# Attention with mixed heads: keys and queries stored once, two heads on the halves of the array

## The chip, the cores and the metric

One core of one Trainium2 chip runs the whole program as one launch. The core has a matrix array (TensorE, PE in the profile; its weight loads are PEld), VectorE (DVE), ScalarE (ACT), GpSimd (POOL), a queue engine that issues transfers (SyncE, SP), and 16 DMA engines. The metric is device time in microseconds, the median of repeated runs. The kernel before takes 1551.23 us (three runs, 1547.59 to 1551.54).

## The reference

Four batches, twelve heads, 448 positions, 64 values a head. Scores are mixed across heads before the softmax, probabilities after it; the result passes through two feed-forward parts.

```
scores = matmul(q, k.T) / 8
scores = einsum('bhij,hg->bgij', scores, w_pre)
attn = exp(scores - max(scores))
attn = attn / (sum(attn) + 1e-9)
attn = einsum('bhij,hg->bgij', attn, w_post)
x = matmul(attn, v)                      # then heads side by side: (1792, 768)
h = x @ w_in                             # 768 -> 2048
x = (h * cos(h)) @ w_out                 # 2048 -> 768
out = (silu(x @ w_gate) * (x @ w_val)) @ w_out2
```

## The kernel before

The 448 query rows of a batch are cut into four chunks of 12, 12, 11 and 10 blocks; a block holds ten query positions for all twelve heads, 120 rows. Work goes by blocks (45 a batch, 180 in all), and for each block there are steps: `premix` multiplies the scores of the block's 120 rows with w_pre (`psm`), `rowmax`, `expo`, `den` and `rec` make the softmax, `norm_hi` and `norm_lo` store it as two half-precision numbers `eh` and `el`, `post` mixes heads again and transposes (`psa`), `at_hi` and `at_lo` store that as high and low half, `at0` and `at1`.

While one chunk goes through these steps, the scores of the next chunk are made head by head (`qk`, tile `pss`), copied to a buffer `s` by ScalarE (`spread`, L201) and sent by a transfer to the rows of `x` where the next chunk's premix reads them (L202). There are three buffers `s` and two banks for `pss`. The product with v (`pv`, tile `psv`) follows seven blocks behind the end of its chunk.

To keep precision, every operand stands as high and low part. For the scores a key tile holds one head: the high part on that head's 64 rows, the low part on the other 64 (`hi_k`, L105, `lo_k`, L110). Queries come from memory twice, on both halves of the rows, so that one matmul over 128 rows sums high and low part of k; the high part of q (`qh`) and its low part (`ql`) each give one matmul (L190), two a head. `qh` is written by a casting transfer from GpSimd's queue (L126) beside the plain one from SP's (L125); `ql` is computed by GpSimd (L135). For the product with v one weight tile holds the high and the low part of one head's v, 128 columns, and eight matmuls a head (L287) leave two sums on two halves of the rows. `pv_out` moves both by ScalarE (L304, L305), adds them on GpSimd (L307) and stores them (L308).

The order on each engine is written out: a plan gives each step a block number, and within a block the kinds of steps stand in the order of one tuple of names, `order`. Steps of the next chunk are put at block s0 + h * (n - 2) // 12 for head h, where s0 is the chunk's first block and n its number of blocks. Engines take their instructions in that order. After the last chunk the feed-forward class takes over; the first pieces of it are planned into the last chunk.

Of the kernel before, what the change touches and what calls it, by code (L numbers as in the profile page):

```python
# [30 lines left out]
def f(ap):  # L31
    return ap.bitcast(F32)


def attention(ctx, tc, qT, kT, vN, mix, xs, ff):
# [9 lines left out]
    p_k = pool("a_k", 13, SB, scores, "right")  # L45
# [54 lines left out]
    def half(h):  # L100
        return slice(64 * (h % 2), 64 * (h % 2) + 64)

    def hi_k(b, h, copy=nc.scalar.copy):
        t = ktiles[b, h] = p_k.tile([128, S], F32R, tag="k", name=f"k_{b}_{h}")
        copy(t[half(h)], raws["k", b, h // 2][half(h)])  # L105

    def lo_k(b, h, eng=nc.gpsimd):

        t = ktiles[b, h]
        eng.tensor_tensor(t[half(h + 1)], raws["k", b, h // 2][half(h)], f(t[half(h)]), op=ALU.subtract)  # L110

    def dma_q(b, c, hh, early=()):

        src = qT[b, c, hh].rearrange("d (e i) -> d e i", e=6)
        if 0 in early or not early:
            hi = p_q.tile([128, 6, 120], F32R, tag="qh", name=f"qh_{b}_{c}_{hh}")
            lo = p_q.tile([128, 6, 120], F32R, tag="ql", name=f"ql_{b}_{c}_{hh}")
            raw = p_q.tile([128, 6, 120], F32, tag="qr", bufs=2, name=f"qr_{b}_{c}_{hh}")
            qtiles[b, c, hh] = hi, lo
            raws["q", b, c, hh] = raw  # L120
        for e in early:
            s = slice(3 * e, 3 * e + 3)
            nc.sync.dma_start(raws["q", b, c, hh][:, s], src[:, s])
        if not early:
            nc.sync.dma_start(raw, src)  # L125
            nc.gpsimd.dma_start(hi, src)  # L126
# [41 lines left out]
    def split_v(b, jc, part):  # L168

        r = raws["v", "r", b, jc]  # L170
        rv = r.rearrange("p (m e d) -> p m e d", e=2, d=D)
        by = vscale[b][0][:112, 1:2]
        if part == 0:
            nc.scalar.activation(r, r, AF.Copy, scale=by)
        elif part == 1:
            t = vtiles[b, jc] = p_v.tile([112, 6, 4, D], F16, tag="v", name=f"v_{b}_{jc}")
            nc.vector.tensor_copy(t[:, :, 0::3], rv)
        else:
            e, t = part - 2, vtiles[b, jc]
            nc.gpsimd.tensor_tensor(t[:, :, 1 + e], rv[:, :, e], t[:, :, 3 * e], op=ALU.subtract)  # L180

    X, SP, SMALL, PM, E, EHL, PA, AT, PV, XO = ({} for _ in range(10))

    def qk(b, c, h, place=(ps_s, "s")):

        n = CH[c]
        hi, lo = qtiles[b, c, h // 6]
        ps = place[0].tile([128, 512], F32, tag=place[1], name=f"pss_{b}_{c}_{h}")
# [4 lines left out]
        SP[b, c, h] = ps  # L193
# [84 lines left out]
    def pv(b, c, h):  # L278

        n = 10 * CH[c]  # L280
        if h % 4 == 0:
            PV[b, c, h // 4] = ps_v.tile([128, 4, 128], F32, tag="pv", name=f"psv_{b}_{c}_{h}")
        ps = PV[b, c, h // 4]
        for jc in range(4):
# [7 lines left out]
    def pv_out(b, c, g4, par):  # L292

        n = 10 * CH[c]
        if par == 0:
            XO[b, c, g4] = p_o.tile(
                [128, 2, n], F32, tag="xo", padded_shape=[128, 2, 120], bufs=3, name=f"xo_{b}_{c}_{g4}"
            ), p_o.tile([128, 2, 120], F32, tag="xt", name=f"xt_{b}_{c}_{g4}")
        x, t = XO[b, c, g4]
        ps = PV[b, c, g4]  # L300
        und = vscale[b][1]
        own = slice(64 * par, 64 * par + 64)
        off = slice(64 - 64 * par, 128 - 64 * par)
        nc.scalar.activation(t[own, :, :n], ps[off, par::2, :n], AF.Copy, scale=und[own])  # L304
        nc.scalar.activation(x[own], ps[own, par::2, :n], AF.Copy, scale=und[own])  # L305
        if par == 1:
            nc.gpsimd.tensor_tensor(x, x, t[:, :, :n], op=ALU.add)  # L307
            nc.sync.dma_start(  # L308
                xs[b][:, 2 * g4:2 * g4 + 2, COFF[c]:COFF[c] + CREAL[c]], x[:, :, :CREAL[c]]
            )  # L310
# [6 lines left out]
    def at(i, fn, *a):  # L317
        plan.setdefault((i, fn.__name__), []).append((fn, a))
# [6 lines left out]
    for ci, (b, c) in enumerate(chunks):  # L325
        n, s0 = CH[c], first[b, c]
        if ci + 1 < len(chunks):
            nb, ncn = chunks[ci + 1]
            for h in range(12):
                i = s0 + h * (n - 2) // 12  # L330
                at(i, qk, nb, ncn, h)
                at(i + 1, spread, nb, ncn, h)
            for hh in range(2 if ci else 0):
                i = s0 - 6 + 4 * hh
                at(i, dma_q, nb, ncn, hh)
                for e in range(2):
# [28 lines left out]
        for h in range(12):  # L365
            i = s0 + n + 7 + h * (nn - 2) // 12
            at(i, pv, b, c, h)
            if h % 4 == 3:
                for par in range(2):
                    at(i + 1 + par, pv_out, b, c, h // 4, par)  # L370
# [4 lines left out]
    order = ("at_hi","l1_part","post","spread","dma_v","w_bits","hidden","den","rowmax","rec","norm_hi","dma_k","x_dma","w_dma","pv_out","at_lo","norm_lo","lo_k","dma_q","max_v","w_shift","lo_q","split_v","x_lo","premix","scale_v","w_split","expo","x_hi","qk","hi_k","pv")  # L375


    with tc.manual_schedule():
        vec, act, pl = nc.vector, nc.scalar, nc.gpsimd
        dma_q(0, 0, 0, range(1))  # L380
        for m in range(6):
            dma_k(0, m, p_fk)
            if m == 1:
                dma_q(0, 0, 0, range(1, 2))
            if m == 3:
                dma_q(0, 0, 1, range(2))
        hi_q(0, 0, 0, 0, vec.tensor_copy)
        lo_q(0, 0, 0, 0, vec)
        for h in range(0, 12, 2):
            for k in (h, h + 1):  # L390
                hi_k(0, k, act.copy if k == 1 else vec.tensor_copy)
            if h == 0:
                hi_q(0, 0, 0, 1, act.copy)
            for k in (h, h + 1):
                lo_k(0, k, pl if k in (3, 5, 9, 11) else vec)
            if h == 0:
                lo_q(0, 0, 0, 1)
            if h == 4:
                for e in range(2):
                    lo_q(0, 0, 1, e)  # L400
            for k in (h, h + 1):
                qk(0, 0, k, ((ps_s, "s"), (ps_a, "a"), (ps_m, "m"))[k % 3])
                spread(0, 0, k, p_fk, 12)
                if k == 3:
                    nc.sync.dma_start(mix_sb, mix)
                if k in (1, 2):
                    hi_q(0, 0, 1, k - 1, act.copy)
# [13 lines left out]
        p_o = pool("a_o", 2)  # L421
# [285 lines left out]
def _layout(inputs):  # L707
# [21 lines left out]
    def bits(w):  # L729
# [4 lines left out]
        "qT": np.concatenate([qT, qT], 3).reshape(B, 4, 2, 128, 720),  # L734
# [31 lines left out]
```

## Time and profile before

| | |
|---|---|
| median of three runs | 1551.23 us |
| profiled execution | 1546.38 us, span 1544.6 us |
| array (PE) busy | 1457.5 us (94%) |
| VectorE busy | 985.5 us (64%) |
| ScalarE busy | 731.2 us (47%) |
| GpSimd busy | 712.8 us (46%) |
| mean granted clock of the array | 0.993 of full speed |

The shares are means over two stages that differ: attention up to about 510 us, where all engines are loaded, and the feed-forward part, where the array is nearly always busy. Rows of a stretch or of a place in time tell more than the totals. The array's matmuls are pipelined, so the shown durations overlap, and the distance between starts is what one costs.

### The profile page before, as it was taken

To read this page: it belongs to the slowest core of one execution; us is meant where nothing else is said; L and a number is where in the kernel's file an instruction comes from. 1 tells how busy PE (TensorE), PEld (TensorE's weight loads), DVE (VectorE), ACT (ScalarE), POOL (GpSimd) and SP (SyncE) were. 2 spreads that over 40 slices of the span, in tenths; PEclk is the share of its full clock that TensorE was granted. 3 is DMA by queue.
4 is the path that set the end of the run, shared out by engine and by line. 5 is a ranking of instruction groups with operands and counts; after the bars stand their busy time and mean duration, and the time that the engine had idled before them with its cause. 6 is when DMAs were issued, how large, how long until landed. Compare 5 with 4: busy or idle time off the path is not lost.

```text
span 1544.6 us, 25392 instructions
## 1 busy us (share of the span) xinstructions
PE 1457.5 (94%) x9346; PEld 1239.7 (80%) x9346; DVE 985.5 (64%) x1966; ACT 731.2 (47%) x1579; POOL 712.8 (46%) x658
## 2 busy tenths in 40 slices
PE   5898898998898899999999999999999999999999
PEld 3566666666666779999999998998998989899898
DVE  6987878887788785757767766833336263542613
ACT  4788888888788773322322323533313131221310
POOL 3888889889787752322423323213213131321310
PEclk9999999999999999999999999999999999999999
DMA  6666567556644541212202211211203030120202
GB/s 205 162 189 177 162 173 199 169 157 196 178 129 142 140 134 60 62 41 62 62 30 73 62 42 41 62 41 53 71 2 102 21 102 21 53 71 1 72 37 108
DMA packets 100589, 149.19 MB, mean 97 GB/s; under 512 B 19856, under 2 KB 82544, under 8 KB 100464
## 3 DMA queue, kind: packets, MB, share of 16 engines
q1 hardware_dynamic: 96432, 137.24, 30.4%
q0 software_dynamic: 4032, 10.32, 2.6%
q8 instruction: 74, 1.21, 0.3%
q14 instruction: 51, 0.42, 0.1%
HBM read 97.81 MB, written 11.01 MB: 70 GB/s over the span
## 4 chain that ended last, share of the span: by engine, by line
PE 68%; DVE 12%; DMA 8%; ACT 6%; issue 3%; POOL 2%; SPq 1%; ACTq 0%; POOLq 0%
PE ph L592 11%; PE ph L593 11%; PE ph L594 11%; PE py L638 8%; PE py L639 8%; PE py L640 8%; DMA x<-s 5%; PE psm L206 4%; PE pss L190 3%; PE psv L287 2%; DVE el L242 2%; DVE sm L211 1%; ACT e L219 1%; POOL l_i L532 1%; DMA qr<-in_qT 1%
## 5 line engine op out<-in xcount | busy, mean ns | idle before, releaser
L616 POOL TENSOR_TENSOR gl<-r,gh 128x448 fp32r<-128x448 f32 x112 | 133.9, 1196 | 495.9 <-ACT gh L615 465.8
L592 PE MATMUL ph<-x,h_i 128*128 128x448 f32 x960 | 352.3, 367 | 0.0
L593 PE MATMUL ph<-x,h_i 128*128 128x448 f32 x960 | 351.1, 366 | 1.2 <-POOL x L572 1.2
L594 PE MATMUL ph<-x,l_i 128*128 128x448 f32 x960 | 351.1, 366 | 0.2 <-POOL l_i L532 0.2
L638 PE MATMUL py<-gh,h_o 128*128 128x448 f32 x672 | 249.7, 372 | 12.2 <-DVE acc L644 7.9
L640 PE MATMUL py<-gh,l_o 128*128 128x448 f32 x672 | 247.5, 368 | 0.6 <-POOL l_o L532 0.6
L639 PE MATMUL py<-gl,h_o 128*128 128x448 f32 x672 | 247.4, 368 | 0.0
L235 POOL TENSOR_SCALAR eh<-e,sm 120x448 f16<-120x448 f32 x180 | 216.4, 1202 | 62.2 <-DVE sm L230 29.0
L644 DVE TENSOR_TENSOR acc<-py,acc 128x448 f32<-128x448 f32 x288 | 176.0, 620 | 88.1 <-PE py L640 87.8
L206 PE MATMUL psm<-x,wpre_sb 120*120 120x448 f32 x360 | 180.9, 585 | 39.8 <-ACT e L219 28.8
L593 PEld LDWEIGHTS ph<-x,h_i 128*128 128x128 f32 x960 | 180.5, 188 | 17.0 <-POOL x L572 1.6
L592 PEld LDWEIGHTS ph<-x,h_i 128*128 128x128 f32 x960 | 180.5, 188 | 15.3 <-issue 0.4
L594 PEld LDWEIGHTS ph<-x,l_i 128*128 128x128 f32 x960 | 180.4, 188 | 15.4 <-POOL l_i L532 0.6
L614 DVE TENSOR_TENSOR r<-ph,r 128x448 f32<-128x448 f32 x48 | 29.9, 623 | 200.7 <-PE ph L594 200.5
L638 PEld LDWEIGHTS py<-gh,h_o 128*128 128x128 f32 x672 | 126.2, 188 | 31.7 <-DVE acc L644 13.3
L532 POOL TENSOR_TENSOR l_i<-f_i,h_i 128x384 fp32r<-128x384 f32 x80 | 87.6, 1102 | 137.8 <-ACT h_i L531 137.8
L242 DVE SCALAR_TENSOR_TENSOR el<-e,sm,eh 120x448 f16<-120x448 f32 x180 | 141.0, 783 | 9.6 <-POOL eh L235 9.6
L615 ACT CAST gh<-r 128x448 fp32r<-128x448 f32 x112 | 63.4, 566 | 174.4 <-DVE r L614 136.4
L255 PE MATMUL psa<-wpost,eh 120*112 120x120 f16 x720 | 126.3, 218 | 14.3 <-DVE at L276 12.9
L640 PEld LDWEIGHTS py<-gh,l_o 128*128 128x128 f32 x672 | 126.4, 188 | 13.2 <-POOL l_o L532 1.4
L639 PEld LDWEIGHTS py<-gl,h_o 128*128 128x128 f32 x672 | 126.4, 188 | 11.3
L190 PE MATMUL pss<-k,qh 128*120 128x448 f32 (+2 forms) x192 | 122.6, 639 | 11.3 <-DVE k L110 7.4
(88 smaller groups left out, 2680.9 us busy)
## 6 DMA issues: line engine op xcount, KB each, us to landing
r_o<-in_w_out SPq DMA_DIRECT2D x56, 384.0 KB
x<-s SPq DMA_DIRECT2D x96, 210.0 KB
r_i<-in_w_in SPq DMA_DIRECT2D x32, 384.0 KB
qh<-in_qT POOLq DMA_DIRECT2D x28, 360.0 KB, 4.9
qr<-in_qT SPq DMA_DIRECT2D x28, 360.0 KB
x<-s SPq DMA_DIRECT2D x48, 192.5 KB
r_i<-in_w_gate SPq DMA_DIRECT2D x24, 384.0 KB
r_i<-in_w_val SPq DMA_DIRECT2D x24, 384.0 KB
```

The costliest lines, as they stand in the source:

```text
L190: nc.tensor.matmul(ps[:10 * n, :S], qq[:, h % 6, :10 * n], ktiles[b, h], start=(i == 0), stop=(i == 1))
L206: nc.tensor.matmul(ps[:120, :S], wpre_sb, X[b, c][:120, k], start=True, stop=True)
L235: nc.gpsimd.tensor_scalar(eh, E[b, c, k], sm[:, 3:4], 1.0, op0=ALU.mult, op1=ALU.mult)
L242: nc.vector.scalar_tensor_tensor(el, E.pop((b, c, k)), sm[:, 3:4], eh, op0=ALU.mult, op1=ALU.subtract)
L592: nc.tensor.matmul(ps, wh, xh, start=(kk == 0), stop=False)
L593: nc.tensor.matmul(ps, wh, xl, start=False, stop=False)
L594: nc.tensor.matmul(ps, wl, xh, start=False, stop=(kk == 5))
L616: nc.gpsimd.tensor_tensor(gl, r, f(gh), op=ALU.subtract)
L638: nc.tensor.matmul(ps, wh, gh[:, e], start=(e == 0), stop=False)
L639: nc.tensor.matmul(ps, wh, gl[:, e], start=False, stop=False)
L640: nc.tensor.matmul(ps, wl, gh[:, e], start=False, stop=(e == 1))
L644: nc.vector.tensor_tensor(acc[:, m], ps, acc[:, m], op=ALU.add)
```

## The change

Keys lie once as a high tile and a low tile of 128 rows, two heads on the halves (`k0`, `k1`), and queries likewise (`q0`, `q1`); queries are read from memory once. For a pair of heads the scores are three products (high with high, low q with high k, high q with low k), each as two matmuls over 64 rows, one a head, on the two halves of the array's rows. The product with v takes three products instead of four (low with low is left out), each as two matmuls with 64 columns, one a head, on the two halves of the array's columns. Both halves of a pair's result so stand where they are stored, `pv_out` is one activation for three pairs, and the addition is gone. The plan goes by pairs, and the cast of the queries' high part (`hi_q`) is now on VectorE.

```diff
-    p_k = pool("a_k", 13, SB, scores, "right")
+    p_k = pool("a_k", 7, SB, scores, "right")
...
+    def hi_k(b, m, copy=nc.scalar.copy):
+        t = ktiles[b, m] = tuple(
+            p_k.tile([128, S], F32R, tag=f"k{z}", name=f"k{z}_{b}_{m}") for z in range(2)
+        )
+        copy(t[0], raws["k", b, m])
+    def lo_k(b, m, eng=nc.gpsimd):
+        hi, lo = ktiles[b, m]
+        eng.tensor_tensor(lo, raws.pop(("k", b, m)), f(hi), op=ALU.subtract)
+    def dma_q(b, c, parts=(slice(0, 6),)):
...
+        for s in parts:
+            nc.sync.dma_start(raws["q", b, c][:, s], src[:, s])
+    def hi_q(b, c, e, copy=nc.vector.tensor_copy):
...
-        for i, qq in enumerate((hi, lo)):
-            nc.tensor.matmul(
-                ps[:10 * n, :S], qq[:, h % 6, :10 * n], ktiles[b, h], start=(i == 0), stop=(i == 1)
-            )
+        for i, (zq, zk) in enumerate(((0, 0), (1, 0), (0, 1))):
+            for e in range(2):
+                r = slice(64 * e, 64 * e + 64)
+                nc.tensor.matmul(
+                    SP[b, c, 2 * m + e][:n, :S], qtiles[b, c][zq][r, m, :n], ktiles[b, m][zk][r],
+                    start=(i == 0), stop=(i == 2),
+                )
...
-            vt = vtiles[b, jc][:, h // 2, 2 * (h % 2):2 * (h % 2) + 2]
-            for z in range(2):
+        prods = [(jc, zv, za) for jc in range(4) for zv, za in ((0, 0), (0, 1), (1, 0))]
+        for i, (jc, zv, za) in enumerate(prods):
+            for e in range(2):
                 nc.tensor.matmul(
-                    ps[:, h % 4, :n].rearrange("p (k i) -> p k i", i=10), vt, AT[b, c][z][:, :, jc * H + h],
-                    start=(jc == 0 and z == 0), stop=(jc == 3 and z == 1),
+                    ps[64 * e:64 * e + 64, m % 3, :n].rearrange("p (k i) -> p k i", i=10),
+                    vtiles[b, jc][:, m, e, zv], AT[b, c][za][:, :, jc * H + 2 * m + e],
+                    start=(i == 0), stop=(i == len(prods) - 1),
                 )
...
-        nc.scalar.activation(t[own, :, :n], ps[off, par::2, :n], AF.Copy, scale=und[own])
-        nc.scalar.activation(x[own], ps[own, par::2, :n], AF.Copy, scale=und[own])
-        if par == 1:
-            nc.gpsimd.tensor_tensor(x, x, t[:, :, :n], op=ALU.add)
+        nc.scalar.activation(x, PV.pop((b, c, g3))[:, :3, :n], AF.Copy, scale=vscale[b][1])
...
-            for h in range(12):
-                i = s0 + h * (n - 2) // 12
-                at(i, qk, nb, ncn, h)
-                at(i + 1, spread, nb, ncn, h)
-            for hh in range(2 if ci else 0):
-                i = s0 - 6 + 4 * hh
-                at(i, dma_q, nb, ncn, hh)
+            for m in range(6):
+                i = s0 + m * (n - 2) // 6
+                at(i, qk, nb, ncn, m)
                 for e in range(2):
-                    at(i + 3 + e, lo_q, nb, ncn, hh, e)
+                    at(i + 1, spread, nb, ncn, 2 * m + e)
+            if ci:
+                at(s0 - 6, dma_q, nb, ncn)
+                for e in range(2):
+                    at(s0 - 3 + e, hi_q, nb, ncn, e)
+                    at(s0 - 2 + e, lo_q, nb, ncn, e)
...
-        for hh in range(2):
-            for e in range(2):
-                hi_q(0, 1, hh, e, act.copy)
-                lo_q(0, 1, hh, e)
+        dma_q(0, 1)
+        for e in range(2):
+            hi_q(0, 1, e)
+            lo_q(0, 1, e)
...
-        "qT": np.concatenate([qT, qT], 3).reshape(B, 4, 2, 128, 720),
+        "qT": qT.reshape(B, 4, 128, 720),
```

On the array, in block 1 of chunk 1 of the second batch, the kernel before has after the premix one head of the next chunk's scores and then a head's product with v (names carry batch, chunk and head or block, then a running number):

```order
L206 MATMUL psm_1_1_1_2845<-x_1_1_2245,wpre_sb_269 120x448
L190 MATMUL pss_1_2_2_2849<-k_1_2_1466,qh_1_2_0_2509 110x448
L190 MATMUL pss_1_2_2_2849<-k_1_2_1466,ql_1_2_0_2510 110x448
L287 LDWEIGHTS v_0_0_574
L287 MATMUL psv_0_3_8_2852<-at0_0_3_1988,v_0_0_574 128x100
L287 LDWEIGHTS v_0_0_574
L287 MATMUL psv_0_3_8_2852<-at1_0_3_1989,v_0_0_574 128x100
```

In the same place the changed kernel has a pair of heads, in turn (`k0` and `q0` are high parts, `k1` and `q1` low ones; `psv_0_3_3` begins with pair 3):

```order
L202 MATMUL psm_1_1_1_2957<-x_1_1_2322,wpre_sb_250 120x448
L186 MATMUL pss_1_2_2_2961<-k0_1_1_1495,q0_1_2_2597 110x448
L186 MATMUL pss_1_2_3_2962<-k0_1_1_1495,q0_1_2_2597 110x448
L186 MATMUL pss_1_2_2_2961<-k0_1_1_1495,q1_1_2_2598 110x448
L186 MATMUL pss_1_2_3_2962<-k0_1_1_1495,q1_1_2_2598 110x448
L186 MATMUL pss_1_2_2_2961<-k1_1_1_1496,q0_1_2_2597 110x448
L186 MATMUL pss_1_2_3_2962<-k1_1_1_1496,q0_1_2_2597 110x448
L284 LDWEIGHTS v_0_0_571
L284 MATMUL psv_0_3_3_2900<-at0_0_3_2049,v_0_0_571 64x100
```

Two matmuls for one head have become six for two heads, which write two banks in turn, and the matmuls with v write 64 rows instead of 128. Blocks without a pair have neither.

On ScalarE, in blocks 2 and 3 of chunk 0 of the same batch, one score copy stood in each block, with two activations that move results out:

```order
L219 ACTIVATE e_1_0_0_2268,sm_1_0_0_2253<-psm_1_0_0_2213,sm_1_0_0_2253 120x448
L268 ACTIVATE at0_0_3_1988<-psa_0_3_6_2232 112x480
L201 COPY s_1_1_2_2303<-pss_1_1_2_2270 120x448
L304 ACTIVATE xt_0_2_1_2313<-psv_0_2_4_2177,und_0_469 64x2x110
L305 ACTIVATE xo_0_2_1_2312<-psv_0_2_4_2177,und_0_469 64x2x110
L219 ACTIVATE e_1_0_1_2322,sm_1_0_1_2307<-psm_1_0_1_2266,sm_1_0_1_2307 120x448
L268 ACTIVATE at0_0_3_1988<-psa_0_3_7_2290 112x480
L201 COPY s_1_1_3_2350<-pss_1_1_3_2324 120x448
```

Now both copies of a pair stand in one block, and a block without a pair has none:

```order
L215 ACTIVATE e_1_0_0_2340,sm_1_0_0_2330<-psm_1_0_0_2296,sm_1_0_0_2330 120x448
L264 ACTIVATE at0_0_3_2049<-psa_0_3_6_2309 112x480
L197 COPY s_1_1_2_2389<-pss_1_1_2_2342 120x448
L197 COPY s_1_1_3_2392<-pss_1_1_3_2343 120x448
L215 ACTIVATE e_1_0_1_2406,sm_1_0_1_2396<-psm_1_0_1_2338,sm_1_0_1_2396 120x448
L264 ACTIVATE at0_0_3_2049<-psa_0_3_7_2376 112x480
L215 ACTIVATE e_1_0_2_2457,sm_1_0_2_2447<-psm_1_0_2_2404,sm_1_0_2_2447 120x448
```

Two copies have moved together in front of one `exp`, and the results of the product with v come out later, as one activation for six heads.

## Rows read from the trace of the kernel before

**Rows 1.** Busy time by stretch: the second batch, and after attention.
```profile
core 0: us, PE busy (x) PEld busy (x) DVE busy (x) ACT busy (x) POOL busy (x), PEclk, DMA share, GB/s
...
147.14:268.32 121.18, 108.52 (x1117) 78.18 (x1114) 98.23 (x242) 103.91 (x247) 106.52 (x101) 1.00 0.62 176
...
510.46:1544.60 1034.14, 1014.80 (x5109) 924.99 (x5106) 571.74 (x971) 321.00 (x613) 296.85 (x263) 1.00 0.20 59
```

**Rows 2.** Who waited for whom, 60 to 510 us: total, times, longest.
```profile
DVE sm L226 <- ACT e L219: 53.8, 70, 3.3
...
PE psm L206 <- ACT e L219: 24.7, 24, 3.4
...
ACT s L201 <- DMA x<-s: 23.6, 17, 3.4
```

**Rows 3.** The array in order of time, one block: start, duration.
```profile
202.47 0.97 PE L206 MATMUL psm<-x,wpre_sb 120*120 120x448 f32 x2
202.93 0.72 PE L190 MATMUL pss<-k,qh 128*110 128x448 f32 x1
203.49 0.37 PE L190 MATMUL pss<-k,ql 128*110 128x448 f32 x1
203.70 0.60 PE L287 MATMUL psv<-at,v 112*128 112x120 f16 x8
204.14 0.22 PE L255 MATMUL psa<-wpost,eh 120*112 120x120 f16 x1
...
204.77 0.97 PE L206 MATMUL psm<-x,wpre_sb 120*120 120x448 f32 x2
205.57 0.59 PE L287 MATMUL psv<-at,v 112*128 112x120 f16 x8
```

**Rows 4.** Longest chain pieces, 60 to 510 us, and a ScalarE copy that waited.
```profile
133.04 7.04 DMA x<-s
164.65 7.99 DMA qr<-in_qT
198.88 6.17 DMA x<-s
...
205.15 0.53 ACT L201 COPY s<-pss 110x448 f32<-110x448 f32 x1 [1.88 <-DMA x<-s]
```

**Rows 5.** Weight loads by shape: busy, mean ns of one, idle before.
```profile
L255 PEld LDWEIGHTS <-eh 120*112 120x112 f16 x720 | 94.1, 131 | 19.2 <-issue 11.5 <-POOL l_i L532 1.9 <-POOL v L180 1.8
L287 PEld LDWEIGHTS <-v 112*128 112x128 f16 x1536 | 82.4, 97 | 42.8 <-issue 42.8
...
L190 PEld LDWEIGHTS pss<-k,qh 128*120 128x120 f32 x96 | 19.2, 200 | 33.7 <-issue 10.6 <-ACT s L201 9.7 <-DVE k L110 6.5
```

**Rows 6.** ScalarE, GpSimd and VectorE by shape: busy, mean ns of one.
```profile
L268 ACT ACTIVATE at<-psa 112x480 f16<-112x480 f32 x180 | 101.5, 564 | 0.5
...
L305 ACT ACTIVATE xo<-psv,und 64x240 f32<-64x240 f32 x48 | 21.9, 456 | 0.6
L105 ACT CAST k<-kr 64x448 fp32r<-64x448 f32 x37 | 20.6, 558 | 2.3 <-DMA kr<-in_kT 1.8
...
L135 POOL TENSOR_TENSOR ql<-qr,qh 128x360 fp32r<-128x360 f32 x63 | 63.4, 1009 | 25.1 <-ACT qh L130 14.8 <-DMA qr<-in_qT 5.3 <-PE psa L257 1.5
L110 POOL TENSOR_TENSOR k<-kr,k 64x448 fp32r<-64x448 f32 x40 | 55.1, 1377 | 6.2 <-issue 2.1 <-DVE k L105 1.1
L126 POOL DMA_DIRECT2D qh<-in_qT x28 | 16.9, 604 | 0.0
L307 POOL TENSOR_TENSOR xo<-xo,xt 128x240 f32<-128x240 f32 x24 | 16.7, 697 | 1.0 <-ACT xo L305 1.0
...
L130 DVE CAST qh<-qr 128x360 fp32r<-128x360 f32 x1 | 0.3, 347 | 2.0 <-DMA qr<-in_qT 2.0
```

**Rows 7.** VectorE in order of time, start of the program.
```profile
30.92 0.95 DVE L147 TENSOR_REDUCE vmx<-vm 112x1 f32<-112x768 f32 x1 [8.18 <-DMA vm<-in_vN]
```

More of the change, by code (lines that the diff above doesn't have):

```diff
@@ L98, in dma_k @@
         raws["k", b, m] = r
[L100 to L126, printed above, removed]
@@ new lines, in lo_k @@
+    def lo_k(b, m, eng=nc.gpsimd):
+        hi, lo = ktiles[b, m]
+        eng.tensor_tensor(lo, raws.pop(("k", b, m)), f(hi), op=ALU.subtract)
+    def dma_q(b, c, parts=(slice(0, 6),)):
+        if parts[0].start == 0:
+            qtiles[b, c] = tuple(
+                p_q.tile([128, 6, 120], F32R, tag=f"q{z}", name=f"q{z}_{b}_{c}") for z in range(2)
+            )
+            raws["q", b, c] = p_q.tile([128, 6, 120], F32, tag="qr", bufs=2, name=f"qr_{b}_{c}")
+        src = qT[b, c].rearrange("d (m i) -> d m i", m=6)
+        for s in parts:
+            nc.sync.dma_start(raws["q", b, c][:, s], src[:, s])
@@ L137, in dma_v, with lo_q @@
+    def hi_q(b, c, e, copy=nc.vector.tensor_copy):
+        s = slice(3 * e, 3 * e + 3)
+        copy(qtiles[b, c][0][:, s], raws["q", b, c][:, s])
+    def lo_q(b, c, e, eng=nc.gpsimd):
+        hi, lo = (t[:, 3 * e:3 * e + 3] for t in qtiles[b, c])
+        eng.tensor_tensor(lo, raws["q", b, c][:, 3 * e:3 * e + 3], f(hi), op=ALU.subtract)
     def dma_v(b, jc, why):
@@ L276, in at_lo, with pv @@
         nc.vector.scalar_tensor_tensor(tl, src, 2.0 ** -4, th, op0=ALU.mult, op1=ALU.subtract)
-    def pv(b, c, h):
+    def pv(b, c, m):
         n = 10 * CH[c]
[L281 to L284, printed above, removed]
-            vt = vtiles[b, jc][:, h // 2, 2 * (h % 2):2 * (h % 2) + 2]
-            for z in range(2):
+        if m % 3 == 0:
+            PV[b, c, m // 3] = ps_v.tile([128, 4, 128], F32, tag="pv", name=f"psv_{b}_{c}_{m}")
+        ps = PV[b, c, m // 3]
+        prods = [(jc, zv, za) for jc in range(4) for zv, za in ((0, 0), (0, 1), (1, 0))]
+        for i, (jc, zv, za) in enumerate(prods):
+            for e in range(2):
@@ L364, in attention @@
         nn = CH[chunks[ci + 1][1]] if ci + 1 < len(chunks) else 12
[L365 to L370, printed above, removed]
+        for m in range(6):
+            i = s0 + n + 7 + m * (nn - 2) // 6
+            at(i, pv, b, c, m)
+            if m % 3 == 2:
+                at(i + 1, pv_out, b, c, m // 3)
     for i, fn, *a in ff.early_plan(first[B - 1, 3]):
@@ L373, in attention @@
         at(i, fn, *a)
-    order = ("at_hi","l1_part","post","spread","dma_v","w_bits","hidden","den","rowmax","rec","norm_hi","dma_k","x_dma","w_dma","pv_out","at_lo","norm_lo","lo_k","dma_q","max_v","w_shift","lo_q","split_v","x_lo","premix","scale_v","w_split","expo","x_hi","qk","hi_k","pv")
+    order = ("at_hi","l1_part","post","spread","dma_v","w_bits","hidden","den","rowmax","rec","norm_hi","dma_k","x_dma","w_dma","pv_out","at_lo","norm_lo","lo_k","dma_q","max_v","w_shift","lo_q","split_v","x_lo","premix","scale_v","w_split","expo","x_hi","qk","hi_k","hi_q","pv")
@@ L378, in attention @@
     with tc.manual_schedule():
         vec, act, pl = nc.vector, nc.scalar, nc.gpsimd
-        dma_q(0, 0, 0, range(1))
-        for m in range(6):
[L382 to L398, printed above, removed]
-                for e in range(2):
[L400 to L407, printed above, removed]
@@ L408, in attention @@
-        for hh in range(2):
-            dma_q(0, 1, hh, range(2))
-        for hh in range(2):
-            for e in range(2):
-                hi_q(0, 1, hh, e, act.copy)
-                lo_q(0, 1, hh, e)
+        dma_k(0, 0, p_fk)
+        dma_q(0, 0, (slice(0, 3),))
+        dma_k(0, 1, p_fk)
+        dma_q(0, 0, (slice(3, 6),))
+        for m in range(2, 6):
+            dma_k(0, m, p_fk)
+        nc.sync.dma_start(mix_sb, mix)
+        places = (ps_s, "s"), (ps_a, "a"), (ps_m, "m")
+        for m in range(6):
+            hi_k(0, m, act.copy if m % 2 else vec.tensor_copy)
+            if m == 0:
+                hi_q(0, 0, 0, act.copy)
+                lo_q(0, 0, 0, vec)
+            lo_k(0, m, pl if m % 2 else vec)
+            if m == 0:
+                hi_q(0, 0, 1, act.copy)
+                lo_q(0, 0, 1, pl)
+            qk(0, 0, m, places)
+            for e in range(2):
+                spread(0, 0, 2 * m + e, p_fk, 12)
@@ L414, in attention @@
+        dma_q(0, 1)
+        for e in range(2):
+            hi_q(0, 1, e)
+            lo_q(0, 1, e)
         wpre_sb = const.tile([120, 120], F32, name="wpre_sb")
@@ L714, in _layout @@
         n, g = CREAL[c], CH[c]
-        part = np.zeros((B, 2, 6, 10 * g, D), q.dtype)
-        part[:, :, :, :n] = q[:, :, COFF[c]:COFF[c] + n].reshape(B, 2, 6, n, D)
-        part = part.reshape(B, 2, 6, g, 10, D).transpose(0, 1, 5, 2, 4, 3)
+        part = np.zeros((B, 6, 2, 10 * g, D), q.dtype)
+        part[:, :, :, :n] = q[:, :, COFF[c]:COFF[c] + n].reshape(B, 6, 2, n, D)
+        part = part.reshape(B, 6, 2, g, 10, D).transpose(0, 2, 5, 1, 4, 3)
         qT[:, c, :, :, :, :10 * g] = part.reshape(B, 2, D, 6, 10 * g)
```

57 lines of the change are left out of this document (21 added, 36 removed).

## The prediction

> **What bounds the kernel now.** I began with busy time by stretch. The 1544.6 us fall into a start, four batches of attention that end at 510.46 us (the second is a row, 121.2 us, so some 485 us for all) and the feed-forward part behind it. In the last part the array is busy for 1014.8 of 1034.1 us, and the change touches none of its lines, so all must happen in the first 510 us. In a batch of 121.2 us no engine is full: array 108.5, ScalarE 103.9, GpSimd 106.5, VectorE 98.2, the DMA engines at 0.62 [rows 1]. Then the list of waits: VectorE stands 53.8 us until ScalarE's `exp` has ended, the array 24.7 us for the same `exp`, ScalarE 23.6 us (17 times) until a spread transfer has freed a buffer [rows 2]. So the engines pass a delay round among them, and the order in time must say which of them paces an undisturbed block.
>
> It is the array. From one `psm` to the next lie 2.30 us without a gap: 0.80 for the premix (204.77 to 205.57, where no qk stands between), 0.43 for the two qk matmuls of a head (1.23 from `psm` to `psv`, less 0.80), 0.44 for the eight matmuls with v of a head, 0.63 for the twelve of `post` [rows 3]. Starts are used here, since the durations overlap. A qk matmul so takes 0.215 us, one with v 0.055. A batch has 45 blocks and 48 heads of each product: 45 x 1.43 + 48 x 0.87 = 106.1 us. The other 15.1 of 121.2 us are disturbed blocks, above all long transfers: the longest pieces of the chain are a spread of 7.04 us and one of queries of 7.99 us [rows 4].
>
> **The change, part by part.** *Scores.* Two heads had four matmuls over 128 rows; now they have six over 64, in turn on the upper and the lower half. Nothing in this trace has two matmuls beside each other, so I bound them from both sides: beside each other 3 x 0.215 = 0.65 us a pair, one after another 6 x 0.215 = 1.29, against 0.86 now. The weight loads of one half must also run beside those of the other: a load takes 0.20 us [rows 5], which fits one to a step of 0.215, not two.
>
> *Product with v.* Two heads had 16 matmuls with 128 columns, now 24 with 64. Beside each other 12 x 0.055 = 0.66 us, one after another 1.32, against 0.88. The load again: 128 columns took 97 ns, 112 columns of the same type 131 ns, and yet the latter keep a step of 0.0525 us (twelve in 0.63) [rows 3, 5]. So the wide load is the quicker one, and 64 columns may not have that speed. The Trainium skill, TensorEngine Tiling (Array Packing), Restrictions, says that splitting the columns switches the fast weight load off; the trace agrees as far as its narrower load is slower. If a load's share of a step goes with its width, two loads of 64 columns ask 2 x 0.0525 x 64/112 = 0.060 us a step, and a pair costs 0.72 us, not 0.66: 1.4 us more a batch. I take 0.66.
>
> For both products I take the lower bound, as the halves share no rows of the array in the one case and no columns in the other, and no operand waits on the other half's result: -0.43 us a pair, 24 pairs a batch, -10.4: array 95.7 us. The upper bound is +0.87 a pair, +20.9: 127.0.
>
> *ScalarE.* Moving results out goes from 48 activations a batch of 0.456 to 8 over 128x360; the nearest rows are that 0.456 (240 elements) and 0.564 (480), so 0.51: 21.9 - 4.1 = -17.8. Key casts go from 12 of 0.558 to 6, of the same 448 elements: -3.3. ScalarE: 103.9 to 83 [rows 1, 6].
>
> *GpSimd.* Low parts of queries 16 to 8 a batch at 1.01 (-8.1), of keys 12 to 6 at 1.377 (-8.3), 12 additions of 0.70 (-8.4) and 8 issues of 0.604 (-4.8) go: 106.5 to 77 [rows 1, 6].
>
> *VectorE* takes on the query casts, 8 a batch. The one such cast in the trace took 0.347; beside GpSimd it may take twice that. I take 0.5: 98.2 to 102 (101 to 104) [rows 1, 6]. The cast waits for the query transfer, issued three blocks (some 6.9 us) earlier; behind it stand the next block's `den` and `rowmax`, for which `exp` waits. A transfer of 7.99 us would cost 1.1 us there. I take nothing, since such lengths should go: queries shrink from four transfers of 360 KB a chunk to one, 4.4 MB a batch of 176 GB/s x 121 us = 21 MB, a fifth [rows 1, 4].
>
> *Start.* Casts of chunk 1's queries now stand on VectorE ahead of the scaling of w_pre, so the first premix waits for that transfer. The copies ahead of it are done sooner, and VectorE idled 8.18 us there for v [rows 7]. I take 0, with 2 us either way.
>
> *The sum.* The largest load is then VectorE's 102 us, the array's 95.7 next. VectorE idles 23.0 us a batch now, mostly behind ScalarE and long transfers. Both get lighter by a fifth, so I keep half of it, 11.5: a batch takes 113.5, 7.7 less. If all of it went, 19 less; if none, 4 more. Four batches: -31 us. The profiled execution took 1546.4 us, so 1515.4; the median of before stands 4.9 higher, so I forecast **1520 us**, with 1503 to 1538 as this case's own range (a third to two thirds of the idle time kept, 2 us for the start).
>
> **Rivals.** *One after another.* The halves don't overlap, in matmuls or in loads, so the change doesn't do what it says. In the array's queue a pair then takes 2.61 us where 1.74 stand now; the array has 127.0 us a batch, and with half of today's 15.1 us of waits 134.5: +13.3 x 4 = +53, **1604 us**. For it speaks that no pair overlaps in this trace and that a step leaves no room for two loads. It decides from about 2.05 us a pair: 106.1 + 24 x 0.31 + 7.5 is today's 121. If only the scores overlap, a pair takes 0.65 + 1.32 = 1.97, the batch 119.2, the time **1543 us**.
>
> *A stop at each change of shape.* A matmul of `post` is shown for 0.22 us at steps of 0.0525, so 0.165 us of it lies under its successors [rows 3]. If the array had to run empty whenever whole, row-halved and column-halved matmuls follow each other, some 20 times a chunk, that is 3.3 us a chunk or 13 a batch: the array is back at 109, and only the relief of the others is left, half of the 15 us of waits: 116.5, -4.7 x 4 = -19, **1532 us**. No row of before has two shapes, so none speaks against it. The Trainium skill, TensorEngine Tiling (Array Packing), Key Properties, states this drain; no run so far shows it.
>
> *Three buffers for spreads that come in pairs.* Before, copy h+3 waited for the transfer of copy h some 2.5 blocks, or 5.8 us, back. Now both heads of a pair are copied in one block; where pairs stand one block apart (11 times a batch, by the division in the plan) it waits for one 2.3 + 0.4 us back. A spread of 6.17 us already held ScalarE for 1.88 us [rows 4]. With some 5 us each, ScalarE stands 2.2 us 11 times: its load is 83 + 24 = 107, more than VectorE's 102. With the same 11.5 us of idle time a batch takes 118.5 us, -2.7 x 4 = -11, **1540 us**. Against it: only 17 copies waited before.
>
> **How the numbers follow.** Side by side as forecast 0.52; a stop at each change 0.13; spread buffers 0.12; only the scores overlap 0.08; one after another 0.15. A measurement of this kernel tells about 0.3% from no change, 4.7 us. Of the first four I count 0.51, 0.12, 0.05 and 0.03 as faster, together 0.71; 0.01, 0.01, 0.05 and 0.03 as the same, 0.10; slower are 0.02 of the third, 0.02 of the fourth and all of the last, 0.19. The range runs from 1497, below which I see 0.05, to 1570, which leaves out most of the last case.
>
> **What would show it.** In order of time, two `pss` of a pair should start almost together, a `psm` with a pair of qk behind it should be followed after 0.80 + 0.65 us, and a pair with v should take 0.66. If the starts are 0.2 and 0.05 us apart, the halves run one after another. Gaps of some 0.17 us at each change of shape mean the stop. VectorE's wait for `exp` should halve; ScalarE's wait for the spread transfer should not exceed 24 us, or the buffers are the price. The forecast is wrong if a batch takes over 118 us.

## The result, and the profile after

The changed kernel takes 1530.08 us (median of four runs, 1526.95 to 1531.48) against 1551.38 us of the kernel before in the same session: a ratio of 0.9857, 95% interval 0.9831 to 0.9883, so 1.4% faster. The forecast was 1520 us with a range of 1497 to 1570. The profiled execution took 1526.95 us, its span 1525.2 us, 19.4 us less than before.

Busy time by stretch, the second batch and what follows attention, in the columns of [rows 1]:

```profile
core 0: us, PE busy (x) PEld busy (x) DVE busy (x) ACT busy (x) POOL busy (x), PEclk, DMA share, GB/s
...
148.31:262.65 114.34, 108.86 (x1356) 69.71 (x1354) 97.39 (x250) 84.47 (x201) 83.56 (x68) 0.99 0.51 148
...
489.78:1525.20 1035.42, 1013.40 (x5181) 923.32 (x5178) 573.47 (x971) 312.55 (x593) 293.36 (x257) 1.00 0.20 59
```

The batch went from 121.2 to 114.3 us, while the array's busy time stayed at 108.9 (108.5 before). It was busy for 90% of the batch and is now for 95%: the array does no less, it waits less. ScalarE lost 19.4 us, GpSimd 23.0, and the transfers fell from 176 to 148 GB/s. From the first premix to the end of attention the four batches take 459.2 us instead of 483.9 (-24.7); the start is 4.1 us longer and the rest 1.3 us, which together make up the 19.4 us.

The array in order of time, in the place that answers to [rows 3] (start, duration; equal instructions in a row are one line):

```profile
211.97 0.97 PE L202 MATMUL psm<-x,wpre_sb 120*120 120x448 f32 x2
212.87 0.85 PE L186 MATMUL pss<-k,q 64*100 64x448 f32 x6
213.65 0.83 PE L284 MATMUL psv<-at,v 112*64 112x120 f16 x24
214.41 0.26 PE L251 MATMUL psa<-wpost,eh 120*112 120x120 f16 x1
214.50 0.22 PE L252 MATMUL psa<-wpost,eh 120*112 120x120 f16 x1
214.56 0.22 PE L253 MATMUL psa<-wpost,el 120*112 120x120 f16 x1
...
215.08 0.97 PE L202 MATMUL psm<-x,wpre_sb 120*120 120x448 f32 x2
215.89 0.22 PE L251 MATMUL psa<-wpost,eh 120*112 120x120 f16 x1
```

Inside the six `pss` the two heads start 3 ns apart; the second two come 0.28 us later and the third two 0.20 (212.87, 213.15, 213.36), so that the first step holds a part of the stop. Inside the 24 `psv` two start at most 5 ns apart, with a step of 0.052 after a first one of 0.079. So the halves do run beside each other. But the pair of scores takes 0.78 us (212.87 to 213.65) where three steps make 0.61, the pair with v 0.76 (213.65 to 214.41) where twelve make 0.63, premix is followed by `pss` after 0.90 us and by `psa` after 0.81 (215.08 to 215.89), and the first `psa` keeps the second waiting 0.09 instead of 0.05. The whole block takes 3.11 us, an empty one 1.43: the two pairs cost 1.68 us, where one pair each cost 0.86 + 0.88 = 1.74 before. In blocks with one pair alone it costs 0.92 (scores) or 0.90 (v). Taken one by one, a change costs 0.09 us behind a premix (0.90 for 0.81), and the rest of the 0.92 or 0.90 lies in the first step of the pair and between the pair and the first two `psa`.

The weight loads of the same stretch show what happens at a change (idle time before the first of a row in brackets):

```profile
212.87 0.45 PEld L186 LDWEIGHTS pss<-k,q 64*100 64x100 f32 x6 [0.66 <-ACT at L264]
213.65 0.67 PEld L284 LDWEIGHTS <-v 112*64 112x64 f16 x24 [0.33 <-issue]
214.41 0.13 PEld L251 LDWEIGHTS <-eh 120*112 120x112 f16 x1
```

The first load of a new shape starts in the same hundredth as its matmul, and ahead of the scores and of v the load side stood idle: no load is taken ahead across these changes. In the kernel before, where no shape changes, the first load of v behind a premix came 0.37 us ahead of its matmul (205.20, with the matmul at 205.57 in [rows 3]). But behind the scores it came with its matmul there too, after 0.24 us of idle loads, and cost nothing:

```profile
203.69 0.44 PEld L287 LDWEIGHTS <-v 112*128 112x128 f16 x8 [0.24 <-issue]
205.20 0.10 PEld L287 LDWEIGHTS <-v 112*128 112x128 f16 x1 [0.19 <-issue]
```

So a late load alone isn't yet a stop. Whether the time goes into emptying the array or into the late load, no run separates.

Loads by shape, beside those of [rows 5]:

```profile
L284 PEld LDWEIGHTS <-v 112*64 112x64 f16 x2304 | 62.0, 109 | 42.9 <-issue 42.4
L186 PEld LDWEIGHTS pss<-k,q 64*120 64x120 f32 x288 | 25.5, 197 | 47.5 <-issue 15.1 <-ACT s L197 14.4 <-ACT k L105 6.5
```

Half the columns load in 109 ns, longer than the 97 of 128 columns; yet two such loads pass in one step of 0.052.

The waits from 60 to 510 us (total, times, longest), as [rows 2]:

```profile
POOL eh L231 <- DVE sm L226: 75.1, 72, 3.8
DVE sm L222 <- ACT e L215: 52.6, 53, 3.4
...
ACT s L197 <- DMA x<-s: 31.3, 26, 3.2
...
PE psm L202 <- ACT e L215: 11.7, 10, 3.0
```

The array's wait for `exp` halved (24.7 to 11.7). VectorE's did not (53.8 to 52.6), and ScalarE waits longer for spread transfers than before, 31.3 us in 26 waits for 23.6 in 17.

ScalarE, GpSimd and VectorE by shape, which answer to [rows 6]:

```profile
L293 ACT ACTIVATE xo<-psv,und 128x360 f32<-128x360 f32 x16 | 9.1, 568 | 1.1 <-PE psv L284 1.1
L105 ACT CAST k<-kr 128x448 fp32r<-128x448 f32 x21 | 11.8, 564 | 0.0
...
L231 POOL TENSOR_SCALAR eh<-e,sm 120x448 f16<-120x448 f32 x180 | 246.7, 1371 | 129.3 <-DVE sm L226 91.0 <-ACT at L264 11.9 <-PE pss L186 9.6
L109 POOL TENSOR_TENSOR k<-kr,k 128x448 fp32r<-128x448 f32 x21 | 24.2, 1153 | 7.3 <-ACT k L105 7.3
...
L238 DVE SCALAR_TENSOR_TENSOR el<-e,sm,eh 120x448 f16<-120x448 f32 x180 | 133.4, 741 | 1.4 <-POOL eh L231 1.4
L124 DVE CAST q<-qr 128x360 fp32r<-128x360 f32 x30 | 10.8, 364 | 17.8 <-DMA qr<-in_qT 17.8
```

GpSimd's `eh` took 1202 ns before and takes 1371 now, though nothing in it was edited: 45 x 0.169 = 7.6 us a batch. The row of before, and two `eh` there with what VectorE did beside them (in order of time):

```profile
L235 POOL TENSOR_SCALAR eh<-e,sm 120x448 f16<-120x448 f32 x180 | 216.4, 1202 | 62.2 <-DVE sm L230 29.0 <-ACT s L201 16.6 <-PE psv L287 6.1
...
206.12 0.63 POOL L235 TENSOR_SCALAR eh<-e,sm 120x448 f16<-120x448 f32 x1
208.26 1.43 POOL L235 TENSOR_SCALAR eh<-e,sm 120x448 f16<-120x448 f32 x1
...
207.95 0.64 DVE L276 SCALAR_TENSOR_TENSOR at<-psa,at 112x480 f16<-112x480 f32 x1
208.51 0.68 DVE L242 SCALAR_TENSOR_TENSOR el<-e,sm,eh 120x448 f16<-120x448 f32 x1
```

The first, beside which VectorE was idle, takes 0.63 us; the second, with `at` and `el` beside it, 1.43. Over all 180 an `eh` has 0.89 us of VectorE's work other than reductions beside it before and 1.09 now, and 12 of them have less than 0.03 us of it before (0.63 us each in the mean), now one. So the longer `eh` goes with more of VectorE's work at the same time.

VectorE at the start, in the place of [rows 7]:

```profile
27.62 0.60 DVE L124 CAST q<-qr 128x360 fp32r<-128x360 f32 x2 [17.28 <-DMA qr<-in_qT]
28.14 0.96 DVE L390 TENSOR_SCALAR wpre_sb<-mix_sb 120x120 f32<-120x120 f32 x1
...
33.40 0.61 DVE L207 TENSOR_REDUCE sm<-psm 120x1 f32<-120x448 f32 x1
```

The scaling of w_pre stands behind a cast that waits for queries, and the first `rowmax` comes at 33.40 instead of 31.79. At the end of the first chunk the delay has shrunk to 1.5 us (60.02 for 58.57).

### The profile page after: what moved, and what is told of

It is laid out like the page before. It is cut to its first block, busy times and chain, and to the rows that moved or that the text cites. A ratio compares the mean times of both kernels' runs of the same rounds, so it can differ in the third digit from the quotient of the medians.

```text
span 1525.2 us, 26832 instructions
## 1 busy us (share of the span) xinstructions
PE 1452.0 (95%) x10306; PEld 1199.3 (79%) x10306; DVE 971.4 (64%) x1982; ACT 652.4 (43%) x1398; POOL 632.0 (41%) x531
## 4 chain that ended last, share of the span: by engine, by line
PE 57%; DVE 4%; POOL 2%; ACT 1%; issue 1%; ACTq 0%; POOLq 0%
PE ph L568 11%; PE ph L567 11%; PE ph L569 11%; PE py L613 8%; PE py L614 8%; PE py L615 8%; POOL l_i L507 1%; DVE f_i L490 1%; DVE f_i L487 1%; DVE f_i L486 1%; ACT f_i L479 1%; ACT h_i L506 0%; POOL l_o L507 0%; DVE f_o L486 0%; DVE r L589 0%
## 5 line engine op out<-in xcount | busy, mean ns | idle before, releaser
L231 POOL TENSOR_SCALAR eh<-e,sm 120x448 f16<-120x448 f32 x180 | 246.7, 1371 | 129.3 <-DVE sm L226 91.0
L202 PE MATMUL psm<-x,wpre_sb 120*120 120x448 f32 x360 | 179.5, 581 | 15.1 <-ACT e L215 14.9
L251 PE MATMUL psa<-wpost,eh 120*112 120x120 f16 x720 | 131.6, 226 | 13.0 <-DVE at L272 10.3
L215 ACT ACTIVATE e<-psm,sm 120x448 f32<-120x448 f32 x180 | 115.2, 640 | 50.5 <-DVE sm L226 48.9
L238 DVE SCALAR_TENSOR_TENSOR el<-e,sm,eh 120x448 f16<-120x448 f32 x180 | 133.4, 741 | 1.4 <-POOL eh L231 1.4
```

The costliest lines, as they stand in the source:

```text
L202: nc.tensor.matmul(ps[:120, :S], wpre_sb, X[b, c][:120, k], start=True, stop=True)
L231: nc.gpsimd.tensor_scalar(eh, E[b, c, k], sm[:, 3:4], 1.0, op0=ALU.mult, op1=ALU.mult)
L238: nc.vector.scalar_tensor_tensor(el, E.pop((b, c, k)), sm[:, 3:4], eh, op0=ALU.mult, op1=ALU.subtract)
L251: nc.tensor.matmul(o, eh[:, j], wpost_sb[0], start=True, stop=False)
```

## The experiments

With the result two theories stood. By the one that I now held, each change of shape stops the array for some 0.15 us, so that the pairs gain nothing there, and the time came from what the other engines and the transfers were relieved of. By the rival, the gain is the overlap of the halves itself, and the relief, which falls on engines that are not the largest, is worth nothing. Ratios are to the kernel before on the same chip, with 95% intervals; the changed kernel's own is 0.9857. The kernel before had medians of 1545.88 to 1551.43 us in these sessions, so ratios are compared, not times.

**Products of one head after those of the other** (the same in `qk`):

```diff
-        for i, (jc, zv, za) in enumerate(prods):
-            for e in range(2):
+        for e in range(2):
+            for i, (jc, zv, za) in enumerate(prods):
```

> The changed kernel with the two loops over heads and products exchanged: all products of the first head, then all of the second, so that neighbours in the array's queue share a half. If the halves ran side by side only because they alternate, a pair's scores go from 3 to 6 steps of 0.203 us and its product with v from 12 to 24 steps of 0.052: +1.23 us a pair, 96 pairs, +118 us, of which the waits of today (some 8 us a batch) may take back up to 30: 1620 to 1650. If the side-by-side starts in the trace are worth nothing, the time stays at 1530.

Measured: 1553.45 us, ratio 1.0051 (1.0032 to 1.0070), 2.0% above the changed kernel and far from 118 us. The block with both pairs in the array, columns as above:

```profile
185.46 0.97 PE L202 MATMUL psm<-x,wpre_sb 120*120 120x448 f32 x2
186.35 0.87 PE L186 MATMUL pss<-k,q 64*110 64x448 f32 x6
187.15 1.11 PE L284 MATMUL psv<-at,v 112*64 112x100 f16 x24
...
188.87 0.97 PE L202 MATMUL psm<-x,wpre_sb 120*120 120x448 f32 x2
```

The six `pss` take 0.80 us, as in the changed kernel (0.78): the second head's three start 10 ns after the first's, although they stand behind them in the queue. In `psv` the second head starts at 187.54, behind nine matmuls of the first, and the block takes 3.41 us (100 columns here; the median of such blocks is 3.56 for 3.11); a block with v alone took 2.78 instead of 2.33. So the array itself takes up work for the idle half from a few places on in its queue: three matmuls ahead cost nothing, twelve are too many. 24 pairs at 0.45 are 10.8 us of array a batch, of which about half lengthens the batches (20.5 us over the four). The halves' overlap is so shown a second time. Both forecasts missed: the overlap doesn't hang on taking turns, but the time didn't stay at 1530 either.

**One more change of shape a block:** `pv` between `post` and `premix`, instead of behind `qk`.

```diff
-    order = (... "x_lo","premix","scale_v","w_split","expo","x_hi","qk","hi_k","hi_q","pv")
+    order = (... "x_lo","pv","premix","scale_v","w_split","expo","x_hi","qk","hi_k","hi_q")
```

> The changed kernel with one kind moved in the order: the product with v now stands between post and premix, not behind qk, so a block that holds both has four changes of the array's shape instead of three. Theory of the stop (a change of shape costs 0.1 to 0.15 us): some 48 blocks hold both, 48 x 0.13 = +6 us, 1536. If a change of shape costs nothing: 1530, within 3 us.

Measured: 1539.84 us, 0.9955 (0.9940 to 0.9970), 1.0% above the changed kernel, more than twice the forecast 0.4%. The array's block:

```profile
209.53 1.01 PE L202 MATMUL psm<-x,wpre_sb 120*120 120x448 f32 x2
210.48 0.86 PE L186 MATMUL pss<-k,q 64*100 64x448 f32 x6
211.27 0.26 PE L251 MATMUL psa<-wpost,eh 120*112 120x120 f16 x1
...
212.03 0.83 PE L284 MATMUL psv<-at,v 112*64 112x120 f16 x24
212.79 1.01 PE L202 MATMUL psm<-x,wpre_sb 120*120 120x448 f32 x2
```

From 209.53 to 212.79 are 3.26 us with four changes, against 3.11 with three, at the same matmuls: +0.15 for one change (0.12 between the medians of all such blocks, 3.23 and 3.11). That is the stop, isolated in the array's block. The batches take 116.0 to 118.1 us (113.0 to 117.7 in the changed kernel). At 0.15 in some 45 blocks the stop is worth 7 us of the 15 that the ratios show; the rest is open, and the product with v now also stands ahead of the next premix.

**Each half of the change alone.** Only keys, queries and scores changed, v as before; and only v changed, scores as before (each takes the other part's functions and plan from the kernel before):

```diff
-    def pv(b, c, m):
+    def pv(b, c, h):
...
-        prods = [(jc, zv, za) for jc in range(4) for zv, za in ((0, 0), (0, 1), (1, 0))]
+        for jc in range(4):
+            vt = vtiles[b, jc][:, h // 2, 2 * (h % 2):2 * (h % 2) + 2]
```

> Only the first half of the change: keys, queries and scores as in the changed kernel; v, the product with v and its output as before. Theory of relief (the array is no faster, the gain is waits that went as ScalarE, GpSimd and transfers got lighter): the transfers of queries, 21 us a batch of GpSimd and 3 of ScalarE go here, so more than half of the gain stays: 1538. If the gain came from the array, this half has as much of it as the other: 1541. If relief of ScalarE is what counts: 1548.

Measured: 1544.32 us, 0.9981 (0.9966 to 0.9997), batches of 117.8 to 121.5.

```diff
-    def qk(b, c, m, places=((ps_s, "s"),)):
+    def qk(b, c, h, place=(ps_s, "s")):
...
-                for e in range(2):
-                    at(s0 - 3 + e, hi_q, nb, ncn, e)
+                i = s0 - 6 + 4 * hh
+                at(i, dma_q, nb, ncn, hh)
```

> Only the second half: scores as before, v, the product with v and its output as in the changed kernel. Theory of relief: ScalarE loses 18 us a batch and GpSimd 8, transfers stay, so the smaller part of the gain: 1544. If relief of ScalarE alone is what counts: 1533. If the array: 1541.

Measured: 1539.61 us, 0.9952 (0.9930 to 0.9974), batches of 115.8 to 122.5. The halves give 0.2% and 0.5%, the whole 1.4%, more than their sum. The theory of relief had the larger share in the scores' half, where most of GpSimd's work and the transfers go; the runs have it the other way round, so the microseconds taken off an engine don't give the size. With the scores' half alone ScalarE is busy for 100.8 of 120 us (148 to 268 us), with v's half alone the transfers move 179 GB/s there; each leaves one of the loads of before in place. That this is why so little is gained is argued, not shown; a plan by pairs that paces the blocks better whatever the loads is a rival that no run tests.

**The relief given back, one engine at a time.** ScalarE gets ten copies a chunk more, GpSimd seven additions, the SP queue three more reads of queries; nobody uses what they write.

```diff
+    def pad_act(b, c, j):
+        t = p_o.tile([128, 3, 128], F32, tag="pad", bufs=1, name=f"pad_{b}_{c}_{j}")
+        nc.scalar.copy(t, mix_sb)
...
+        for j in range(10):
+            at(s0 + j, pad_act, b, c, j)
```

> The changed kernel with ScalarE's relief given back: ten copies of 128x384 a chunk (some 0.5 us each, 21 us a batch, one a block) whose result nothing reads. Theory of relief: ScalarE's share of the 25 us gained in attention comes back, 1538 to 1546 if ScalarE is the one that counted, under 1534 if it was transfers or GpSimd. If the gain came from the array: under 1534.

Measured: 1536.53 us, 0.9908 (0.9878 to 0.9938), half a per cent above the changed kernel, between the two forecasts; ScalarE has 99.1 us in a batch of 115.2, so that of the 19.4 us that it lost 14.6 are back.

```diff
+        nc.gpsimd.tensor_tensor(t, mix_sb, mix_sb, op=ALU.add)
...
+        for j in (0, 1, 3, 4, 6, 7, 9):
+            at(s0 + j, pad_pool, b, c, j)
```

> The changed kernel with GpSimd's relief given back: seven additions of 128x384 a chunk (some 1.05 us each, 29 us a batch) whose result nothing reads. Theory of relief: 1538 to 1546 if GpSimd is the one that counted, under 1534 if not. If the gain came from the array: under 1534.

Measured: 1541.19 us, 0.9946 (0.9921 to 0.9972), 0.9% above; GpSimd has 102.6 us in a batch of 116.2, so that of its 23.0 us 19.0 are back.

```diff
+    def pad_q(b, c, j):
+        t = p_q.tile([128, 720], F32, tag="pad", bufs=2, name=f"pad_{b}_{c}_{j}")
+        nc.sync.dma_start(t, qT[b, c])
...
+                for j, lag in enumerate((6, 2, 2)):
+                    at(s0 - lag, pad_q, nb, ncn, j)
```

> The changed kernel with the transfers given back: three more readings of a chunk's queries, 360 KB each, whose result nothing reads, one six and two two blocks before the chunk, all on SP's queue. Theory of relief: 1538 to 1546 if transfers are what counted, under 1534 if not. If the gain came from the array: under 1534.

Measured: 1562.27 us, 1.0086 (1.0057 to 1.0115), 2.3% above the changed kernel and slower than before. Its waits from 60 to 510 us:

```profile
DVE sm L226 <- ACT e L219: 76.4, 59, 4.1
ACT s L201 <- DMA x<-s: 57.9, 31, 5.1
```

Same bytes as before (148.5 MB for 149.2), and every gain is gone: ScalarE's wait for spread transfers goes from 31.3 to 57.9 us, and VectorE's for `exp`, which stands behind those copies on ScalarE, from 52.6 to 76.4. Of the three loads given back this one costs most, and by these waits it passes through the spread buffers; no run joined it with a fourth buffer. Before, half of these reads went by GpSimd's queue; here all lie in SP's, and 2.3% is more than the whole gain. The three prices add up to 3.7%; they are no shares of the gain, as the work given back stands at other places than the work that went. They show that the path is sensitive to each of the three loads, which the rival denied.

**Four spread buffers**, first in the changed kernel, then in the one before:

```diff
-    p_s = pool("a_s", 3, SB, scores, "right")
+    p_s = pool("a_s", 4, SB, scores, "right")
```

> The changed kernel with four spread buffers instead of three. Theory of the buffers (pairs one block apart wait for a transfer one block back, which holds ScalarE 31 us in 26 waits, and through exp the array): most of these waits go, -6 to -12 us against the changed kernel, a ratio to the kernel before of 0.978 to 0.982. If the waits lie beside other work: no change, 0.986.

Measured: 1514.6 us, 0.9798 (0.9783 to 0.9812), 0.6% below the changed kernel and the fastest of all. The second batch, and a wait from 60 to 510 us:

```profile
142.16:253.49 111.33, 106.86 (x1357) 68.27 (x1354) 98.69 (x249) 83.88 (x201) 82.86 (x68) 1.00 0.53 152
```

```profile
DVE sm L222 <- ACT e L215: 20.5, 37, 1.3
```

ScalarE's wait for spread transfers is down to 0.4 us, and VectorE's for `exp` is 20.5 us instead of 52.6. So that wait was for `exp` held up by copies held up by transfers. The array is busy for 96% of the batch.

> The kernel before, with four spread buffers instead of three and nothing else changed. By my theory (the spread transfers' buffers cost each kernel the waits that it shows on them, and the paired blocks of the changed kernel bring more of these): before shows 23.6 us of ScalarE's waits on spread transfers in 17 waits, against 31.3 in 26 of the changed kernel, whose fourth buffer gave 0.6%; so before gains a little less, 3 to 8 us, a ratio of 0.995 to 0.998, and the changed kernel with four buffers (0.980) stays some 1.5% ahead. By the rival (what the change relieved was only the spread transfers' lateness, which a fourth buffer cures alone) before with four buffers comes to 0.980 to 0.986, and the change adds nothing to it.

Measured: 1539.4 us, 0.9964 (0.9944 to 0.9984). Four buffers give the kernel before 0.4%, so the change with four is still 1.7% ahead (0.9798 / 0.9964, from two chips). The longest waits there, 60 to 510 us, for comparison:

```profile
DVE sm L226 <- ACT e L219: 34.0, 57, 1.2
ACT e L219 <- DVE sm L230: 32.0, 35, 2.4
```

Its spread waits are down to 0.2 us too; what the change gains beyond them isn't in the buffers.

**The start.** Casts of chunk 1's queries behind the preparation of w_pre and w_post:

```diff
         dma_q(0, 1)
-        for e in range(2):
-            hi_q(0, 1, e)
-            lo_q(0, 1, e)
         wpre_sb = const.tile([120, 120], F32, name="wpre_sb")
...
+        for e in range(2):
+            hi_q(0, 1, e)
+            lo_q(0, 1, e)
```

> The changed kernel with the casts of chunk 1's queries moved behind the preparation of w_pre and w_post on VectorE. In the changed kernel the first premix starts at 30.6 us instead of 26.6, its first rowmax ends 34.0 instead of 32.4. Theory that VectorE's queue there costs: first premix near 26 us, 2 to 4 us less, a ratio of 0.983 to 0.984. If the transfers of v bind the start anyway: under 1 us.

Measured: 1526.43 us, 0.9876 (0.9857 to 0.9896): no gain. VectorE there:

```profile
28.95 0.60 DVE L124 CAST q<-qr 128x360 fp32r<-128x360 f32 x2 [6.44 <-DMA qr<-in_qT]
30.01 0.95 DVE L140 TENSOR_REDUCE vmx<-vm 112x1 f32<-112x768 f32 x1 [0.45 <-DMA vm<-in_vN]
30.88 0.61 DVE L207 TENSOR_REDUCE sm<-psm 120x1 f32<-120x448 f32 x1
```

The first `rowmax` comes 2.5 us earlier, the first premix 3.6 (27.0 for 30.6), and the second chunk only 0.7 (59.3 for 60.0): the first batch got longer, 122.2 us for 117.7. The 4 us at the start were not on the path.

**Fewer changes of shape.** Pairs with v put into blocks that have a pair of scores, 77 instead of 45 blocks with both:

```diff
+    with_qk = [first[bc] + m * (CH[bc[1]] - 2) // 6 for bc in chunks[:-1] for m in range(6)]
...
-            i = s0 + n + 7 + m * (nn - 2) // 6
+            i = slots[b, c][m]
```

> The changed kernel with the product with v placed in the blocks that have a pair of scores, wherever the buffers allow (some 77 of 96 pairs instead of some 45 stand in a shared block; the last three chunks are as before). Theory of the stop: a shared block costs 1.69 us for both pairs, two separate ones 0.92 + 0.90, so 32 x 0.13 = -4 us, a ratio of 0.983. If more uneven blocks (3.12 and 1.43 us) make others wait: no gain, or some us lost.

Measured: 1535.03 us, 0.9936 (0.9922 to 0.9950), 0.8% above the changed kernel. Full blocks follow each other at 3.1 us, and many of the empty ones take 1.6 to 2.1 us instead of 1.43 (median 1.78, in the changed kernel 1.52): there the array waits, and what it saved in changes is lost. Which engine paces these blocks was not followed up.

**Four buffers, the start and the alignment together:**

> The three before together: four spread buffers, the start in the other order, the product with v beside the scores. If they add up: -12 to -18 us against the changed kernel, a ratio of 0.974 to 0.978. If all of them lie beside the same waits, not under 0.982.

Measured: 1519.95 us, 0.9829 (0.9811 to 0.9847), 0.3% above the four buffers alone, not clear of the noise (the intervals meet). Start and alignment together gain nothing with four buffers either.

## Why the prediction was right, and where it was not

The time, its sign and the range held (1530 in 1497 to 1570, faster). The likeliest case did not occur as told; the rival of a stop at each change of shape, 1532 us, did. That the forecast of 1520 still came within 10 us is luck in part: two errors in its sum cancel, as told below.

**The step that failed** is "for both products I take the lower bound ... -0.43 us a pair, 24 pairs a batch, -10.4: array 95.7 us". It measures about nothing: 45 x 1.43 + 24 x 0.92 + 24 x 0.90 less some 11 shared changes of 0.13 are 106.6 us a batch, for 106.1 before. The matmuls run beside each other with the steps that I took (0.203 for 0.215, 0.052 for 0.055), so the bound was right for them; what was left out is the changes, two for a pair alone, three for two pairs together: (0.92 - 0.61) / 2 = 0.15, (0.90 - 0.63) / 2 = 0.14, (1.68 - 0.61 - 0.63) / 3 = 0.15. I had worked out 0.165 and 20 a chunk for the rival, and gave it 0.13 since no row of before had two shapes. The Trainium skill, TensorEngine Tiling (Array Packing), Key Properties, states this drain; the trace agrees in that each change costs time, 0.15 us in the mean. I should have put the stop into the main sum at the price that [rows 3] gave.

**The load of 64 columns** was feared to need 0.060 us a step. It takes 109 ns, but the step is 0.052: no cost.

**ScalarE** was to come to 83 us and has 84.5. `pv_out` takes 0.57 us instead of 0.51, which is 0.5 us a batch; the other 1.0 is open.

**GpSimd** was to come to 77 and has 83.6: what I counted is gone, but `eh` got longer by 7.6 us a batch, which I had not seen coming: more of it runs beside VectorE's work.

**VectorE** was to come to 102 and has 97.4. In this batch the eight casts take 3.5 us (4.0 in the sum), and `el` takes 0.8 and the casts of v 1.7 us less than before; the last 1.8 us are open.

**The sum.** I kept half of VectorE's 23 us of idle time; it kept 17.0 (114.3 - 97.4). 97.4 + 17.0 stands where 102 + 11.5 stood, two errors that cancel: -6.8 us for this batch against -7.7. The text also said that VectorE's wait for `exp` should halve; it is 52.6 us for 53.8. VectorE is not what bounds the batch; the array is, with 106.6 of 114.3 us, and its waits fell from 15.1 to 7.7 us. That is "half of the 15 us of waits" of the rival.

**Three spread buffers.** The text said that a wait over 24 us would make them the price. It is 31.3, and a fourth buffer takes 0.6% off. The mechanism is there; its size is 31.3 us of waits in the whole of attention and 12.6 us of span (1525.2 to 1512.6 with four), not 2.2 us for 11 pairs in each of four batches (97 us).

**One after another** is refuted, in matmuls and loads, by starts 3 ns apart.

**The start**: 0 with 2 either way was taken; the first premix comes 4.1 us later, the end of the first chunk 1.5, and moving the casts away gained nothing.

What stays open is how the 24.7 us divide among ScalarE, GpSimd and the transfers: each given back costs time, the two halves of the change alone give little, and no run gives shares. That the array's own load stayed (106.6 us for 106.1) and its waits fell is shown; which relief took the waits away is argued.

## What to carry to other kernels

Two heads on the halves of the array do run at once, but a change between whole, row-halved and column-halved matmuls costs about as much as a short pair saves: put long runs of one shape together, and count the changes before the products. When an engine waits for another that waits for a buffer, a buffer more is the cheapest experiment; here it gave 0.6%. A load that goes from the engines that are not the largest may still shorten the path, when all of them pass one delay round.

## What the runs showed of the hardware

- A change of shape between matmuls costs 0.13 to 0.15 us in the mean, and 0.09 behind a premix. The next shape's first weight load isn't taken ahead of it: it starts with its matmul, after 0.66 us of idle loads behind a premix, 0.33 behind scores.
- Matmuls for the other half of the array need not stand in turn: behind three of the first half the other's start 10 ns later, behind twelve they start after nine.
- A load of 64 columns takes 109 ns, one of 128 columns 97; two of 64 still pass in a step of 0.052 us.
- GpSimd's `eh` takes 0.63 us with VectorE idle beside it, 1.43 with `at` and `el` beside it.
